# Block attention and a feed-forward layer on one core: score and product tiles of one PSUM bank each, and four smaller edits of the plan

## The chip, the cores and the metric

The kernel runs on 1 core of one Trainium2 chip. The metric is device time in microseconds. The time before is 644.97 us, the median of 3 runs (643.79 to 647.47).

## The reference

Two stages follow each other. The first is attention with a local window and block summaries, over 4 batches, 8 heads, 768 positions and 64 features; the second is a feed-forward layer on the 3072 tokens that come out.

```python
block, window = (32, 16)
k_sum = k.reshape(B, H, nb, block, D).max(axis=3)
v_sum = v.reshape(B, H, nb, block, D).mean(axis=3)
scores_l = where(|i - j| < window, scale * q @ k.T, -1e9)
scores_s = scale * q @ k_sum.T + log(block)
a = softmax(concat([scores_l, scores_s]))          # 1e-9 is added to the sum
x = a @ concat([v, v_sum])                         # then (tokens, 512)
h = x @ w_in                                       # 512 -> 2048
g = h * erf(softplus(h))
out = g @ w_out                                    # 2048 -> 512
```

Everything is float32.

## The kernel before, in words

**Tiling.** The 3072 tokens go in 6 chunks of 512. A chunk needs 4 quads of attention (a quad is one pair of heads over 512 tokens, 24 quads in all, numbered `qd`) and 4 periods of the feed-forward layer (a period is 512 of the 2048 inner features, 24 periods in all, numbered `k`; `g = k % 4` is the group of inner features). Attention for quad `k + 4` or so runs inside period `k`, so that TensorE always has feed-forward work beside it. Multiplications of the feed-forward layer are made in three passes: both operands are split into a high and a low part of type fp32r, and high x high, high x low and low x high are added in PSUM.

**Attention of one quad.** `scores` (line 543) fills two PSUM banks, one for each head of the pair; `softmax` (line 581) has VectorE add the mask (line 589, both banks in one instruction) and take the maximum, ScalarE the exponentials with their sums (line 605), and VectorE normalise (line 621); `transp` (line 627) transposes eight 128 x 120 pieces on TensorE into the same two banks, and ScalarE copies both to SBUF in one instruction (line 639); `av` (line 650) multiplies by the values; `xsplit` or `xsplit_fast` splits the result into high and low parts.

**The feed-forward layer in periods 0 to 7.** `mm1` makes `h`, `hout` copies it, then come the activation (softplus; in the first four periods tanh and a logarithm), `erfs` (line 883, the erf, two instructions of 128 x 1024), `gsplit` (line 888: the product at 898, the high part, the low part at 905) and `mm2` (line 910), which multiplies period `k - 1`'s `g` by `w_out` while period `k` is being made. In periods 4 to 7 the erfs are told to come after that period's exponentials (line 1145).

**From period 8 on.** `products` (line 792) makes `h` with fewer multiplications, after Strassen: seven block products, P1 to P7, for each of two halves `n`, from weights, sums of weight blocks (`add_up`) and sums of token blocks (`tsplit`). A job of `products` is six matmuls of 256 columns. The jobs go out in the order P1a P1b P2a P2b P6a P5a P6b P5b P7a P3a P7b P3b P4a P4b, where the last letter is the half: a for the first, b for the second. The first half's results stand in two PSUM tiles of one bank, `h0` and `h1`; the second half's in one PSUM tile of two banks, `pa` (its banks are called pA and pB in the plan). In a pair the first bank takes P2, P5 and P3, the second P1, P6, P7 and P4. Results are copied or added to `hc` as they come: out1, out6, out5, out7 (line 858), out3 (line 861) and out4. In the profile a job of the first half appears as `ha` or `hb`, one of the second half as `pa`.

**Weights.** Sums of weight blocks are made once in periods 5 to 7, in the order of groups 1, 2, 3, 0 (`add_up`, line 387): eight instructions of 128 x 512 for a group (lines 394 and 397), each on VectorE or GpSimd as the plan finds it free; ScalarE and VectorE then split them (403 and 406), and they are stored to device memory. From period 7 on they come back by `get_sums` (line 428, 1 MB each), and the split `w_out` by `get` (line 369, 1 MB each): four such transfers in a period, through a ring of five SBUF slots.

**What sets the order.** Each step is put down as an operation with a cost for each engine that can do it and with names that it reads and writes (`Plan.add`, line 62). `Plan.order` (line 103) is a list scheduler: it takes the engine that can start first and, of the operations that are ready there, the one with the smallest key. The key is a due time, to which a table (`TUNE`, line 46) adds a number for operations 0 to 463; for some operations the table also names the engine. TensorE may take an operation out of turn up to 60 places ahead, as long as its place is below 330, and after that follows the program. `hold` puts off the moment at which a transfer counts as ready in the plan. The instructions of each engine, and of SyncE, which issues almost all transfers, are written out in the planned order, and each engine runs its own list in that order. The semaphores between engines are added afterwards by the tile framework, from the tiles that instructions read and write.

**Draining.** Every fourth period `evac` (line 932) copies a finished chunk from the four output banks to SBUF, on ScalarE alone, and SyncE stores it. Three of the four homes of these copies are the SBUF rows into which `load_nat` loads keys and values for the block summaries.

## Time and profile before

| | |
|---|---|
| runs | 643.79, 644.97, 647.47 us |
| profiled execution, its own time | 646.77 us |
| its span, first to last instruction | 645.0 us |
| mean granted TensorE clock | 0.995 |
| VectorE busy | 432.1 us (67%) |
| ScalarE busy | 406.7 us (63%) |
| GpSimd busy | 39.7 us (6%) |
| moved by DMA | 150.23 MB, 233 GB/s on average |

Everything below the second row is from the profiled execution. A page of the profile has the busy time of each engine, and for each group of instructions their count, mean duration and the idle time of the engine before them, with what ended it. In the profile PE is TensorE's matmuls, PEld its weight loads (which overlap the matmuls), DVE is VectorE, ACT ScalarE, POOL GpSimd and SPq the queue of SyncE. A line such as `PE pa L808 <- DVE hc L861` says that a matmul of line 808 that writes `pa` waited for an instruction of VectorE at line 861 that writes `hc`; a number in brackets at the end of a timeline row is the engine's idle time before it. Line 278 is the helper that copies, so it appears for many tiles. The recorded duration of a matmul includes its way through the array; how often matmuls start is what counts for time, and for those of 256 columns that is every 0.12 us where nothing waits.

### The profile page before, as it was taken

The numbers are of one execution on the slowest core, as the hardware profiler recorded it, in microseconds if no ns is written. First come the engines' busy times: TensorE is split into PE (matmuls) and PEld (weight loads), VectorE is DVE, ScalarE is ACT, GpSimd is POOL, SyncE is SP. The second block draws the span as 40 slices with busy tenths as digits, with TensorE's granted clock in tenths as the row PEclk, the third lists the DMA queues.
The fourth block names the chain that finished last, engine by engine and source line by source line (L and its number), as shares of the span: only waits on it lengthen the run. The fifth ranks groups of instructions, "written<-read, shape, count | busy, mean of one in ns | idle before, by whom it ended". The sixth has DMA issues, their size and how long they took to land.

```text
span 645.0 us, 12021 instructions
## 1 busy us (share of the span) xinstructions
PE 622.7 (97%) x4840; PEld 522.6 (81%) x4840; DVE 432.1 (67%) x607; ACT 406.7 (63%) x804; POOL 39.7 (6%) x68
## 2 busy tenths in 40 slices
PE   7999999999899998999989999999999999999997
PEld 5776558888688787888879889898888898889886
DVE  4999999745898984865658656557646475424442
ACT  5679977887968684664564674574675555552450
POOL 2011010100132310000000000000000000000000
PEclk9999999999899998999999999999999999999999
DMA  9998948734675978788756776666587555574611
GB/s 318 257 381 289 347 163 268 249 109 143 228 275 171 351 246 323 251 296 277 272 171 225 273 259 217 244 218 216 216 271 256 190 181 184 196 258 147 240 74 65
DMA packets 36843, 150.23 MB, mean 233 GB/s; under 512 B 3956, under 2 KB 9396, under 8 KB 24244
## 3 DMA queue, kind: packets, MB, share of 16 engines
q1 hardware_dynamic: 36212, 148.95, 67.4%
q8 instruction: 38, 0.62, 0.4%
q10 hardware_dynamic: 576, 0.52, 0.2%
q14 instruction: 17, 0.14, 0.1%
HBM read 124.13 MB, written 23.07 MB: 228 GB/s over the span
## 4 chain that ended last, share of the span: by engine, by line
PE 78%; DVE 11%; DMA 5%; ACT 3%; issue 1%; SPq 0%; DVEq 0%; ACTq 0%
PE ops L922 31%; PE pa L808 12%; PE h L763 11%; PE hb L808 5%; PE ha L808 5%; PE ops L918 4%; PE px L660 3%; PE pa L635 3%; PE pa L564 2%; DMA out<-rows 2%; DVE hc L861 1%; DVE hc L898 1%; DMA rows<-k_nat 1%; DMA rows<-v_nat 1%; DVE hc L858 1%
## 5 line engine op out<-in xcount | busy, mean ns | idle before, releaser
L922 PE MATMUL ops<-w,gh 128*128 128x512 f32 x704 | 229.7, 395 | 0.0
L922 PEld LDWEIGHTS ops<-w,gh 128*128 128x128 f32 x704 | 132.8, 189 | 27.2 <-ACT gh L278 0.2
L922 PE MATMUL ops<-w,gl 128*128 128x512 f32 x352 | 137.6, 391 | 1.0 <-DVE gl L905 1.0
L898 DVE TENSOR_TENSOR hc<-wt,hc 128x1024 f32<-128x1024 f32 x44 | 55.3, 1273 | 69.6 <-ACT wt L886 69.6
L1169 ACT ACT_TABLE_LOAD x76 | 97.5, 1283 | 1.4
L763 PE MATMUL h<-xh,w 128*128 128x512 f32 x256 | 86.9, 405 | 0.3 <-ACT hc L278 0.3
L922 PEld LDWEIGHTS ops<-w,gl 128*128 128x128 f32 x352 | 66.3, 188 | 13.6 <-DVE gl L905 1.3
L278 ACT COPY hc<-hb 128x256 f32<-128x256 f32 x35 | 13.1, 373 | 85.9 <-PE hb L808 50.1
L763 PEld LDWEIGHTS h<-xh,w 128*128 128x128 f32 x256 | 48.6, 190 | 12.7 <-ACT hc L278 1.5
L605 ACT ACTIVATE pr<-pr,stats 128x120 f32<-128x120 f32 x128 | 48.8, 382 | 8.6 <-DVE stats L614 8.4
L905 DVE TENSOR_TENSOR gl<-hc,gh 128x1024 fp32r<-128x1024 f32 x44 | 53.5, 1222 | 0.3
L763 PE MATMUL h<-xl,w 128*128 128x512 f32 x128 | 50.2, 393 | 0.0
L886 ACT ACTIVATE wt<-wt 128x1024 f32<-128x1024 f32 x48 | 50.0, 1058 | 0.3
L278 DVE CAST gh<-hc 128x1024 fp32r<-128x1024 f32 x40 | 27.8, 697 | 23.5 <-PE ops L922 23.2
L808 PE MATMUL pa<-w,ws 128*128 128x256 f32 x288 | 41.0, 287 | 0.8 <-DVE hc L278 0.8
L527 POOL COPY kw<-ksum 128x96 f32<-128x96 f32 (+1 forms) x28 | 16.1, 590 | 397.9 <-DMA kw<-k_win 270.6
L808 PEld LDWEIGHTS pa<-w,ws 128*128 128x128 f32 x288 | 37.4, 194 | 1.3 <-DVE hc L278 1.2
L808 PE MATMUL hb<-w,ws 128*128 128x256 f32 x192 | 29.1, 288 | 4.3 <-ACT hc L278 2.7
L278 ACT CAST xh<-px 128x512 fp32r<-128x512 f32 (+1 forms) x20 | 10.2, 512 | 36.0 <-PE px L660 36.0
L874 ACT ACTIVATE wt<-hc 128x1024 f32<-128x1024 f32 x32 | 32.1, 1052 | 0.2
L808 PEld LDWEIGHTS hb<-w,ws 128*128 128x128 f32 x192 | 25.9, 196 | 4.7 <-ACT hc L278 2.9
L918 PE MATMUL ops<-a32s,gw 128*128 128x512 f32 x64 | 29.2, 595 | 0.0
(168 smaller groups left out, 1099.0 us busy)
## 6 DMA issues: line engine op xcount, KB each, us to landing
w<-dr SPq DMA_DIRECT2D x36, 1024.0 KB
ws<-ds SPq DMA_DIRECT2D x30, 1024.0 KB
kw<-k_win SPq DMA_DIRECT2D x20, 480.0 KB
rw<-w_in SPq DMA_DIRECT2D x8, 1024.0 KB
rw<-w_out SPq DMA_DIRECT2D x8, 1024.0 KB
dr<-w SPq DMA_DIRECT2D x8, 1024.0 KB
ds<-ws SPq DMA_DIRECT2D x8, 1024.0 KB
vw<-v_win SPq DMA_DIRECT2D x20, 384.0 KB
```

The source lines that it names most:

```text
L278: e.copy(o, i) if e is nc.scalar else e.tensor_copy(o, i)
L605: nc.scalar.activation(s["pr"][:, j], s["pr"][:, j] if qd >= MQ else s["sc"][j // NI][:, i * NK:(i + 1) * NK], AF.Exp, scale=0.125, bias=s ...
L635: nc.tensor.transpose(tp[0:NK, a, i * 128:(i + 1) * 128], s["pr"][:, NI * a + i], ident)
L763: nc.tensor.matmul(hs[k, f][:, 0:T], lhsT=w[m], rhs=xt[ch, cc][x], start=(cc == 0 and n == 0), stop=(cc == 3 and n == 2))
L808: nc.tensor.matmul(shape, lhsT=w[m], rhs=y[l], start=first and c == 0 and i == 0, stop=c == 1 and i == 2, skip_group_check=True)
L874: nc.scalar.activation(wt[k, n], hc[k, n], AF.Softplus)
L886: act(0.96, lambda n=n: nc.scalar.activation(wt[k, n], wt[k, n], AF.Erf, scale=-1.0 if k < SOFT else 1.0), [s], [s], table=("sig",), after ...
L898: e.tensor_tensor(hc[k, n], wt.pop((k, n)), hc[k, n], op=ALU.mult)
L905: e.tensor_tensor(gs[k, n][1], hc.pop((k, n)), f32(gs[k, n][0]), op=ALU.subtract)
L918: nc.tensor.matmul(os_[ch, t], lhsT=x[0][:, i % 2, t * 128:(t + 1) * 128], rhs=w32["o", g, i // 2][:, i % 2], start=first, stop=last)
L922: nc.tensor.matmul(os_[ch, t], lhsT=x[y][:, i % 2, t * 128:(t + 1) * 128], rhs=w[m], start=first and n == 0, stop=last and n == 2)
L1169: nc.scalar.preload_act_table_set(sets[o["load"]])
```

## The change

Five edits are made together. (1) `pa` becomes two PSUM tiles of one bank each, pA and pB, for scores, transposes and the second half's products. The mask is then added in two instructions and the transposed pieces are copied in two; the plan's costs for these steps go from 1.07 to 1.2 and from 0.9 to 1.1. The first job in the second half's second bank claims that bank alone in the plan, not both. (2) The sums of weight blocks are made by VectorE alone for groups 0 and 2 and by GpSimd alone for groups 1 and 3, with a planned cost of 1.5 on GpSimd in place of 1.3. (3) The two kinds of streamed weights, `get` and `get_sums`, have a hold of 2.0 in place of 0. (4) `evac` may run on ScalarE or VectorE, with costs of 0.59 and 0.69 in place of 0.45. (5) The erfs of periods 4 to 7 are no longer told to wait for the exponentials. The table of keys stays as it is.

```diff
@@ -63,7 +63,6 @@
 
 
         n, deps = len(self.ops), set(after)
-        r, w = ([y for x in z for y in (("pA", "pB") if x == "pa" else (x,))] for z in (r, w))
         for x in r:
             deps.update(self.last.get(x, ()))
         for x in w:
@@ -203,7 +202,7 @@
         return t if len(shape) == 2 else t.rearrange("p (a b) -> p a b", a=shape[1]) if len(shape) == 3 else t.rearrange("p (a b c) -> p a b c", a=shape[1], b=shape[2])
 
     def ps(name, tag):
-        return psum.tile([128, 2, 512] if tag == "pa" else [128, 512], F32, name=name, tag=tag)
+        return psum.tile([128, 512], F32, name=name, tag=tag)
 
     ident = sb([128, 128], F32, "ident")
     make_identity(nc, ident)
@@ -287,6 +286,7 @@
     FIRST = {4: 9, 5: 8, 6: 12, 7: 13}
     LATER = {0: 12, 1: 13, 2: 9, 3: 8, 4: 9, 5: 8}
     ROUND = (12, 13, 11, 9, 8)
+    ON_DVE = (0, 2)
     SUMS, TURN, RAW_X = 11, (12, 13), 10
     kept = {}
 
@@ -374,7 +374,7 @@
             t = slot(n, [128, 2, 2, 512], F32R, "w")
             whl[u] = t[:, 0], t[:, 1]
             nc.sync.dma_start(out=f32(t), in_=dr[m])
-        dma(1049, go, [f"d{m}"], frees(n), hold=0.0)
+        dma(1049, go, [f"d{m}"], frees(n), hold=2.0)
 
 
     w_at = {("o", m // 2, m % 2): n for m, n in FIRST.items()}
@@ -408,7 +408,7 @@
         def out_(n):
             dr["s", g, n] = dram.tile([128, 2, 4, 2, 128], F32, name=f"ds{g}{n}", tag=f"ds{g}{n}")
             nc.sync.dma_start(out=dr["s", g, n], in_=f32(s["hl", n]))
-        sum_eng = {"DVE": 0.66, "POOL": 1.3}
+        sum_eng = {"DVE": 0.66} if g in ON_DVE else {"POOL": 1.5}
         for i, (r, j) in ((0, (0, 0)), (3, (1, 1)), (2, (0, 1)), (1, (1, 0))):
             on(sum_eng, lambda e, i=i, r=r, j=j: whole(e, i, r, j), w[r:r + 1] + ([] if i == 0 else [f"w{SUMS}"]), (frees(SUMS) if i == 0 else []) + [f"s{i}"])
         for o, x, y, op in ((3, 2, 3, ALU.add), (2, 0, 2, ALU.subtract), (0, 3, 0, ALU.subtract), (1, 1, 0, ALU.subtract)):
@@ -431,7 +431,7 @@
         def go():
             t = w_sum[g, n] = slot(m, [128, 2, 4, 2, 128], F32R, "ws")
             nc.sync.dma_start(out=f32(t), in_=dr["s", g, n])
-        dma(1049, go, [f"ds{g}{n}"], frees(m), hold=0.0)
+        dma(1049, go, [f"ds{g}{n}"], frees(m), hold=2.0)
 
 
     rows = sb([128, 2 * S], F32, "rows")
@@ -540,15 +540,16 @@
             dma(100 if n == NB else 50, lambda b=b, js=js, n=n: nc.sync.dma_start(out=s["vw"][LW:NK, js], in_=vsum[vrows[b % 2], p:p + 1, :].to_broadcast([NS, n, 128])),
                 [f"vsum{b % 2}{p}"], ["vw"])
 
-    def scores(qd, banks=("pa",)):
+    PA = ("pA", "pB")
+
+    def scores(qd, banks=PA):
 
         s = st[qd]
 
         def mask():
             for n in banks:
                 tiles[n] = ps(n, n)
-            s["sc"] = [tiles["pa"][:, 0], tiles["pa"][:, 1]] if banks == ("pa",) else [tiles[n] for n in banks]
-            s["both"] = tiles["pa"] if banks == ("pa",) else None
+            s["sc"] = [tiles[n] for n in banks]
             m0 = mask_at[qd // NP % 3]
             for sc in s["sc"] if qd < MQ else []:
 
@@ -578,7 +579,7 @@
             pe(0.96, lambda: keys(near), [f"qf{qd}", f"kf{qd}"], banks)
             pe(0.5, lambda: keys(lambda r, j: [(LW, ksum[r, 0, qd])]), [f"qf{qd}", f"ksum0{qd}"], banks)
 
-    def softmax(qd, banks=("pa",)):
+    def softmax(qd, banks=PA):
         s = st[qd]
         m0 = mask_at[qd // NP % 3]
         mk = mask_sb[:, m0:m0 + NI]
@@ -586,8 +587,8 @@
 
         def add(e):
             t = s["pr"] = sb([128, 2 * NI, NK], F32, "pr")
-            e.tensor_tensor(t.rearrange("q (a i) c -> q a i c", a=2), s["both"][:, :, 0:NI * NK].rearrange("q a (i c) -> q a i c", i=NI),
-                            mk.unsqueeze(1).to_broadcast([128, 2, NI, NK]), op=ALU.add)
+            for a in range(2):
+                e.tensor_tensor(t[:, NI * a:NI * a + NI], s["sc"][a][:, 0:NI * NK].rearrange("q (i c) -> q i c", i=NI), mk, op=ALU.add)
 
         def red(e):
             s["mx"] = stat(0, par)
@@ -609,7 +610,7 @@
             e.tensor_scalar(s["rs"], s["sm"], 1e-9, None, op0=ALU.add)
 
         if qd >= MQ:
-            on({"DVE": 1.07}, add, banks, [pr])
+            on({"DVE": 1.2}, add, banks, [pr])
         on({"DVE": 1.06 if qd >= MQ else 1.14}, red, [pr] if qd >= MQ else banks, [f"mx{par}"])
         on({"DVE": 0.07}, lambda e: e.tensor_scalar(s["mx"], s["mx"], -0.125, None, op0=ALU.mult), [f"mx{par}"], [f"mx{par}"])
         s["exps"] = act(3.02 if qd >= MQ else 2.7, exps, [f"mx{par}"] + ([] if qd >= MQ else list(banks)), [pr, f"sm{par}"], table=("log", "exp"))
@@ -629,16 +630,17 @@
         pr = "pr" if qd >= NP else f"pr{qd}"
 
         def go():
-            tp = tiles["pa"] = s["tp"] = ps("pa", "pa")
+            s["tp"] = [ps(n, n) for n in PA]
             for a in range(2):
                 for i in range(NI):
-                    nc.tensor.transpose(tp[0:NK, a, i * 128:(i + 1) * 128], s["pr"][:, NI * a + i], ident)
+                    nc.tensor.transpose(s["tp"][a][0:NK, i * 128:(i + 1) * 128], s["pr"][:, NI * a + i], ident)
 
         def cp():
             s["pt"] = sb([NK, 2, T], F32, "ptr", "pt")
-            nc.scalar.copy(s["pt"], s["tp"][0:NK, :, 0:T])
-        pe(0.95, go, [pr], ["pa"])
-        act(0.9, cp, ["pa"], ["pt"])
+            for a in range(2):
+                nc.scalar.copy(s["pt"][:, a], s["tp"][a][0:NK, 0:T])
+        pe(0.95, go, [pr], PA)
+        act(1.1, cp, PA, ["pt"])
 
     turned = [0]
 
@@ -787,7 +789,7 @@
         act(0.96 if k < SOFT else 1.06, fn, [f"hc{s}"], [f"wt{s}"], table=("sig", "exp") if k < SOFT else ("soft",))
 
     def pair_banks(n):
-        return ("h0", "h1") if n == 0 else ("pA", "pB")
+        return ("h0", "h1") if n == 0 else PA
 
     def products(k):
         ch, g = divmod(k, NG)
@@ -795,11 +797,7 @@
 
         def go(n, x, what, z, first):
             if (n, x) not in where_:
-                if n == 0:
-                    where_[0, x] = ps("h" + x, pair_banks(0)["ab".index(x)])
-                else:
-                    t = tiles["pa"] = ps("pa", "pa")
-                    where_[1, "a"], where_[1, "b"] = t[:, 0], t[:, 1]
+                where_[n, x] = ps("h" + x, pair_banks(n)["ab".index(x)])
             o = where_[n, x][:, z]
             for c in range(2):
                 w, y = what(n, c)
@@ -837,7 +835,7 @@
 
         def job(name, n):
             x, what, z, first, r = jobs[name]
-            pe(0.72, lambda: go(n, x, what, z, first), r(n), pair_banks(n) if (name, n) == ("P1", 1) else [pair_banks(n)["ab".index(x)]])
+            pe(0.72, lambda: go(n, x, what, z, first), r(n), [pair_banks(n)["ab".index(x)]])
 
         def bank(n, x):
             return where_[n, x]
@@ -932,10 +930,10 @@
     def evac(ch, t):
         home = HOMES[t]
 
-        def cp():
+        def cp(e):
             tiles["ob", t] = rows[:, t * C:t * C + C] if t < 3 else sb([128, C], F32, "ob", "mask_h")
-            nc.scalar.copy(tiles["ob", t], os_.pop((ch, t)))
-        act(0.45, cp, [f"o{t}"], home)
+            copy(e, tiles["ob", t], os_.pop((ch, t)))
+        on({"ACT": 0.59, "DVE": 0.69}, cp, [f"o{t}"], home)
         dma(262, lambda: nc.sync.dma_start(out=out[ch * T + t * 128:ch * T + (t + 1) * 128], in_=tiles["ob", t]), home)
 
     def evac_last(t):
@@ -952,7 +950,7 @@
         on({"DVE": 0.4}, lambda e: go(e, 1), [f"o{t}"], after=[len(P.ops) - 1])
 
 
-    banks = [("pa",), ("h0", "h1"), ("o0", "o1"), ("h0", "h1")]
+    banks = [PA, ("h0", "h1"), ("o0", "o1"), ("h0", "h1")]
     idle = ps("idle", "o3")
 
     def busy(n):
@@ -1142,7 +1140,7 @@
             for r in range(2):
                 get(2 * (k % NG) + r, turn())
         logs(k)
-        erfs(k, [st[qs]["exps"]] if NG <= k < FAST and qs < NQ else [])
+        erfs(k, [])
         if k and g == 0:
             for t in range(NT):
                 evac(ch - 1, t)
```

## The prediction

> **What bounds the kernel now.** I read the page's busy times first.
>
> ```profile
> PE 622.7 (97%) x4840; PEld 522.6 (81%) x4840; DVE 432.1 (67%) x607; ACT 406.7 (63%) x804; POOL 39.7 (6%) x68
> ```
>
> TensorE bounds it: 645.0 us of span hold 22.3 us in which no matmul is recorded. None of the edits takes matmuls away, so only such gaps, and stretches at a lower clock, can be won. Next the waits of TensorE's weight loads, which show a gap sooner than the matmuls (columns: total us, times, longest).
>
> ```profile
> PEld pa L808 <- DVE hc L861: 10.1, 14, 1.2
> PEld hb L808 <- ACT hc L278: 2.9, 1, 2.9
> PEld hb L808 <- DVE hc L278: 1.7, 1, 1.7
> ```
>
> The first is nearly half of it all and comes back 14 times: a product of the second half waits for out3. The others come once each, and the table by stretch (us, PE busy, PEld, DVE, ACT, POOL, clock, DMA share, GB/s) shows where.
>
> ```profile
> 30.00:60.00 30.00, 30.00 (x213) 21.36 (x209) 29.48 (x37) 25.10 (x54) 4.07 (x4) 1.00 0.94 339
> 160.00:185.00 25.00, 22.54 (x150) 17.94 (x149) 20.67 (x28) 23.62 (x45) 5.42 (x5) 0.93 0.73 258
> 215.00:245.00 30.00, 27.30 (x195) 22.88 (x193) 28.25 (x36) 21.84 (x39) 3.83 (x4) 1.00 0.85 313
> 245.00:271.40 26.40, 26.08 (x207) 23.32 (x208) 15.72 (x23) 16.06 (x35) 0.35 (x1) 0.94 0.82 277
> 474.40:499.30 24.90, 24.43 (x206) 21.70 (x206) 14.33 (x22) 14.88 (x33) 1.25 (x1) 1.00 0.78 266
> ```
>
> An early stretch (30 to 60) has no gap. Around 160 to 185 TensorE stands for 2.46 us and runs the rest at a mean clock of 0.93 over the stretch; at 215 to 271.4 it is 2.70 + 0.32 us and 0.94. A late period loses about half a microsecond and nothing else. So there are two places to win: the wait in every late period, and two stalls in periods 4 to 8.
>
> **Part 1: the split tile.** One late period in order of time:
>
> ```profile
> 478.53 0.88 PE L808 MATMUL hb<-w 128*128 128x256 f32 x6
> 478.80 0.42 DVE L858 TENSOR_TENSOR hc<-pa,hc 128x256 f32<-128x256 f32 x1 [0.82 <-PE pa L808]
> 479.14 0.68 DVE L861 TENSOR_TENSOR hc<-pa,hc 128x512 f32<-128x512 f32 x1
> 479.87 0.98 PE L808 MATMUL pa<-w 128*128 128x256 f32 x6 [0.47 <-DVE hc L861]
> ```
>
> P4a (`hb<-w`) starts at 478.53, and its six matmuls at 0.12 us leave TensorE free at 479.25. P4b writes bank pB. The last reader of pB is out7 (line 858), which ends at 479.22. Yet P4b starts at 479.87, 0.05 us after out3 (line 861) ended at 479.82, and out3 reads pA. That is a wait for a reader of the other bank, and it costs 0.62 us. Whether two tiles of one bank have it can be read off the first half, which has such tiles already:
>
> ```profile
> 328.07 0.88 PE L808 MATMUL hb<-w 128*128 128x256 f32 x6
> 328.62 0.68 DVE L861 TENSOR_TENSOR hc<-ha,hc 128x512 f32<-128x512 f32 x1
> ```
>
> There P4a starts 0.55 us before the out3 of its own half, so nothing holds it. After the change P4b then waits for out7 alone. In the late period out7 ends 0.03 us before TensorE is free, and it can only come sooner: it now starts after P3b, the last writer of the old tile, and will need P7b alone. I leave no rest of this wait. Its price is 10.1 us less the 0.05 us by which the weight load's gap exceeds the true loss (0.67 in this row's period against 0.62), 14 times: 10.1 - 0.7 = **9.4 us**, with 8.7 (14 x 0.62) and 10.1 as bounds.
>
> What the split adds are second instructions:
>
> ```profile
> L639 ACT COPY ptr<-pa 120x1024 f32<-120x1024 f32 x24 | 24.1, 1006 | 5.0 <-PE pa L635 3.6 <-PE px L660 1.4
> L278 ACT COPY hc<-h 128x512 f32<-128x512 f32 x22 | 12.6, 594 | 13.3 <-PE h L763 13.2
> L589 DVE TENSOR_TENSOR pr<-pa,mask_sb 128x960 f32<-128x960 f32 x16 | 18.4, 1151 | 6.8 <-PE pa L564 6.8
> L660 PEld LDWEIGHTS px<-ptr,vw 120*64 120x64 f32 x640 | 20.3, 138 | 4.4 <-issue 2.9 <-ACT w L278 0.8 <-ACT pr L605 0.4
> ```
>
> The copy becomes two of some 0.59 us: 1.19 - 1.01 = 0.18 us, 24 times, 4.3 us of ScalarE. The mask becomes two of about 0.65 us (out3's 0.68 us is for 512 columns, these are 480): 0.15 us, 16 times, 2.4 us of VectorE. The last row shows that the product after the copy never waits for line 639, so the matmuls put between them cover it; uncovered it would be 4.3 us. Queued behind the longer mask on VectorE are the maximum and the next results' copies, in late periods with VectorE busy 14 of 25 us. I charge 0.4 us, for the first quads, where little lies between; bounds 0 and 4.3.
>
> **Part 2: the erfs of periods 4 to 7.** ScalarE, and what TensorE made of it, in period 4:
>
> ```profile
> 149.11 1.06 ACT L781 ACTIVATE wt<-hc 128x1024 f32<-128x1024 f32 x1 [0.64 <-DVE hc L278]
> 156.30 0.59 ACT L937 COPY rows<-ops 128x512 f32<-128x512 f32 x1 [1.89 <-PE ops L922]
> 163.12 2.00 ACT L886 ACTIVATE wt<-wt 128x1024 f32<-128x1024 f32 x2
> 168.56 0.79 PE L922 MATMUL ops<-w,gl 128*128 128x512 f32 x1 [0.95 <-DVE gl L905]
> ```
>
> The softplus is done at 150.2, the erf starts at 163.1, after the exponentials, and five microseconds later TensorE gets the low part of `g` that it stands for. In between ScalarE idled (1.89 us in the second row alone). Without the order the planner finds the erfs ready some 10 us sooner, and a list scheduler takes what is ready. The stall is worth 2.46 us and, by the clock, up to 0.07 x 25.0 = 1.75 us: 4.2 us at most, nothing at least. I take **3.0**, since the two readings of one slow stretch overlap. A greedy order may run the first erf between the two softplus and pay two more table loads in a period; in period 4 the idle time of ScalarE covers them. Period 7 is the second stall:
>
> ```profile
> 225.70 1.06 ACT L781 ACTIVATE wt<-hc 128x1024 f32<-128x1024 f32 x1
> 230.29 1.05 ACT L403 CAST ws<-sums 128x1024 fp32r<-128x1024 f32 x1 [2.24 <-DVE sums L397]
> 239.01 2.01 ACT L886 ACTIVATE wt<-wt 128x1024 f32<-128x1024 f32 x2
> 245.32 0.98 PE L808 MATMUL hb<-w,ws 128*128 128x256 f32 x6 [2.73 <-ACT hc L278]
> ```
>
> It is the same pattern, 12 us from softplus to erf, but here VectorE is busy 28.25 of 30 us, so an earlier erf meets a full queue. The stall is worth 2.70 + 0.32 + 0.06 x 26.4 = 4.6 us. I take **1.5**: a third, because VectorE has to work off the same list by the same time.
>
> **Part 3: sums by one engine.** Of 32 instructions GpSimd has 12 now, and gets 16:
>
> ```profile
> L394 POOL TENSOR_TENSOR sums<-w 128x512 f32<-128x512 f32 x7 | 10.7, 1539 | 31.8 <-DVE ws L406 18.1 <-DVE w L352 13.7
> L397 POOL TENSOR_TENSOR sums<-sums 128x512 f32<-128x512 f32 x5 | 8.2, 1634 | 9.8 <-DVE sums L397 9.6
> 211.09 4.37 POOL L397 TENSOR_TENSOR sums<-sums 128x512 f32<-128x512 f32 x2 [2.11 <-DVE sums L397]
> 211.99 4.55 DVE L898 TENSOR_TENSOR hc<-wt,hc 128x1024 f32<-128x1024 f32 x2
> L898 DVE TENSOR_TENSOR hc<-wt,hc 128x1024 f32<-128x1024 f32 x44 | 55.3, 1273 | 69.6 <-ACT wt L886 69.6
> ```
>
> VectorE loses four of about 0.68 us (out3's duration for as many columns), 2.7 us less. But the rows at 211 and 212 show both engines slow beside each other: two of line 898 take 4.55 us, against 2 x 1.27 by their mean. So a GpSimd instruction beside VectorE costs it about 1.0 us, and four more cost 4.0. Net it is -2.7 to +1.3 us of VectorE; I set it at nothing and carry 4.0 as a bound on what reaches TensorE.
>
> **Part 4: streamed weights later, and the drain.** SyncE and the first use of what it fetched, and one transfer of 256 KB from the chain of waits:
>
> ```profile
> 427.44 0.34 SPq L433 DMA_DIRECT2D ws<-ds  x1
> 428.88 8.87 SPq L376 DMA_DIRECT2D w<-dr  x2
> 447.85 0.88 PE L808 MATMUL hb<-w,ws 128*128 128x256 f32 x6
> 277.01 8.71 DMA out<-rows
> ```
>
> The sums asked for at 427.44 are used after 447.85. A megabyte takes about 3.9 us at the 266 GB/s of the late stretch, and even a small transfer in a crowd took 8.71, so more than 10 us stay. A hold moves these issues behind other transfers in SyncE's queue, not behind anything that TensorE stands for: **0**, bounds -1 and +1. The drain, free to take VectorE, releases the rows sooner, and late rows made this:
>
> ```profile
> 293.67 0.95 DVE L452 TENSOR_REDUCE vs_sum<-rows 128x24 f32<-128x768 f32 x1 [3.54 <-DMA rows<-v_nat]
> 296.55 0.98 PE L808 MATMUL hb<-w,ws 128*128 128x256 f32 x6 [1.54 <-DVE hc L278]
> ```
>
> The reduction held VectorE's queue for 3.54 us, and TensorE lost 1.54. I take 0.5 of it; bounds 1.7 and nothing.
>
> **The sum.** 9.4 + 3.0 + 1.5 + 0.5 - 0.4 = 14.0 us. The profiled execution took 646.77 us, 1.77 more than its span, and becomes 632.8. It lies 1.80 above the median of the runs, so the median becomes 644.97 - 14.0 = **631.0 us**.
>
> **The rivals.** *The wait goes, the stalls only move.* A planner that is given other costs writes another order for periods 4 to 11, and DVE's 28.25 of 30 us speak for a stall of the same size elsewhere. Then only 9.4 less 0.4, 9.0, is left: 644.97 - 9.0 = 636.0 us. Chance 0.24.
>
> *VectorE and GpSimd in each other's way.* Group 3 on GpSimd alone is eight instructions in a chain, 12.6 us at the mean of the twelve (18.9 / 12 = 1.58) and 17.5 at the 2.19 of the row at 211.09, and group 0 queues behind it, where VectorE is full. If all of the 4.0 us lands on TensorE and nothing is won in the middle, it is 644.97 - 9.0 + 4.0, that is 640.0 us. Chance 0.06. The Trainium skill, in SBUF — State Buffer, under "Who interferes with whom", states that a VectorE instruction with two SBUF inputs and a GpSimd instruction that reads SBUF shut each other out for a whole instruction. By that rule, the two rows at 211 and 212 agree: both sides were stretched.
>
> *The split changes no wait.* If the semaphores were still set by the pair, all that part 1 wins is lost, and 3.0 + 1.5 + 0.5 - 0.4 = 4.6 is won: 640.4 us. The row at 328.07 speaks against it. Chance 0.03.
>
> *Slower: the new order opens gaps in the stretch that has none.* Copies and masks cost more in the plan from the first quad on, and an early stretch now has 30.00 of 30.00 us. A stall of the kind at 160 to 185 costs 4.2 us with its clock. The 9.0 us of part 1 pay for two; three make 12.6 - 9.0 = 3.6 us more than now, and from there on the kernel is slower: 648.6 us. Against it: the table of keys and the steps themselves stay. Chance 0.05.
>
> **How the numbers follow.** The forecast has the remaining 0.62. The range starts at 644.97 - 10.1 - 4.2 - 4.6 - 1.7 + 0.4, about 625 us, with every bound on the good side, and ends at 640, which takes in the first rival and reaches the second; beyond lie the slow rival and the third. A measurement of this kernel can tell about 0.5%, 3.2 us, from no change. Faster by more than that (below 641.7) are the forecast, the first rival and most of the next two: 0.91; within it 0.04; slower 0.05.
>
> **What would show it.** The row PEld pa <- DVE hc L861 is gone or below 1 us in total, P4b follows P4a by 0.72 us, and late periods last 24.3 in place of 24.9. The erf of period 4 starts before the exponentials, and stretch 160 to 185 has a clock above 0.97. Line 639 has 48 copies of about 0.59 us with no TensorE wait on them. The prediction is wrong if P4b waits for another reader, or if periods 4 to 8 hold more than 5.5 us of gaps (now 2.46 + 2.70 + 0.32).

## The result and the profile after

The changed kernel takes 628.73 us, the median of 4 runs (626.72 to 631.60). The kernel before, on the same chip, takes 645.04 us (643.79 to 647.47). The ratio is 0.9746, with a 95% interval from 0.9698 to 0.9794: 16.3 us faster. The profiled execution took 629.01 us, with a span of 627.2 us and a clock of 0.997; the four runs differ by the clock that they were granted, 1.000 for 626.72 us, 0.997 for 628.44 and 629.01, 0.995 for 631.60. Lines have moved by one to three: the products are now line 806 (808 before), out3 is 859 (861), out7 856 (858), the erf 884 (886), the copy helper 277 (278), the output products 920 (922).

The busy times of the changed kernel, from its page:

```profile
PE 618.2 (99%) x4840; PEld 520.9 (83%) x4840; DVE 440.3 (70%) x634; ACT 409.6 (65%) x820; POOL 46.4 (7%) x72
```

TensorE now lacks 9.0 us of its span (627.2 - 618.2); before it lacked 22.3. The waits of its weight loads in the changed kernel (total us, times, longest), the largest that has a releaser and the only one of a product that is over 0.2 us:

```profile
PEld ops L920 <- DMA w<-dr: 2.9, 1, 2.9
PEld ha L806 <- DVE w L743: 1.0, 1, 1.0
```

The row with 14 waits and 10.1 us is gone, and so are both waits of `hb` for copies of `hc`. The first row is new: an output product that waited 2.9 us for a weight transfer. In place of `pa`, the products now write `ha` and `hb` in both halves. The two product jobs that the prediction followed, in a late period of the changed kernel's timeline:

```profile
465.35 0.42 DVE L856 TENSOR_TENSOR hc<-hb,hc 128x256 f32<-128x256 f32 x1
465.80 1.60 PE L806 MATMUL hb<-w 128*128 128x256 f32 x12
466.00 0.69 DVE L859 TENSOR_TENSOR hc<-ha,hc 128x512 f32<-128x512 f32 x1 [0.23 <-PE ha L806]
```

P4a and P4b are one row of twelve matmuls without a break, 1.60 us long, and out3 runs beside them from 466.00 to 466.69. The seventh of them, the first of P4b, starts at 466.52, before out3 has ended. In the row that the prediction shows of before, P4a started at 478.53 and P4b ended at 480.85: 2.32 us for the same work. That is 0.72 us a period. The table by stretch of the changed kernel (us, PE busy, PEld, DVE, ACT, POOL, clock, DMA share, GB/s):

```profile
30.00:60.00 30.00, 29.86 (x206) 21.06 (x206) 29.57 (x37) 24.19 (x50) 2.74 (x4) 1.00 0.92 338
160.00:185.00 25.00, 25.00 (x170) 20.62 (x169) 21.54 (x29) 21.81 (x41) 10.40 (x9) 1.00 0.67 232
215.00:245.00 30.00, 28.98 (x221) 25.10 (x219) 26.80 (x39) 22.56 (x42) 2.95 (x3) 1.00 0.85 289
245.00:271.40 26.40, 23.90 (x188) 20.95 (x189) 16.86 (x29) 15.21 (x34) 0.84 (x1) 0.94 0.84 296
461.00:485.20 24.20, 24.20 (x207) 21.67 (x206) 14.70 (x24) 14.79 (x35) 0.63 (x1) 1.00 0.78 268
```

The early stretch stayed full but for 0.14 us. The stall of period 4 is gone, with its clock. The stall between 215 and 271 is not: it is 1.02 + 2.50 us of gap there, 3.02 before, and the clock of the stretch from 245 on is 0.94 again. A late period is 24.20 us and full. In period 4 the first erf now stands between the two softplus and both stand ahead of the exponentials (the last row is the first exponential's sum):

```profile
150.26 1.06 ACT L884 ACTIVATE wt<-wt 128x1024 f32<-128x1024 f32 x1
155.26 1.06 ACT L884 ACTIVATE wt<-wt 128x1024 f32<-128x1024 f32 x1
157.93 0.19 ACT L606 ACTIVATION_READ_ACCUMULATOR pr<-pr,stats 128x1 f32 x1
```

The new stall, first on TensorE, then in the chain of waits of the changed kernel:

```profile
247.50 0.50 PE L920 MATMUL ops<-w,gh 128*128 128x512 f32 x1 [2.73 <-DMA w<-dr]
```

```profile
237.67 1.15 DVE ws L406
238.87 8.58 DMA w<-dr
```

A part of `w_out` is fetched into the ring's slot 11. That slot holds the weight sums of group 0 until their second low part is split off (line 406), which ends at 238.82. SyncE issues the transfer at 238.87, and it lands 8.58 us later, while TensorE stands. In the kernel before the same transfer was issued at much the same time, 239.59, but TensorE stood for the erf then, and needed the weights only later.

### The profile page after: what moved, and what is told of

Its sections match the earlier page's. It is cut to its first block, busy times and chain, and to the rows that moved or that the text cites. A ratio compares the mean times of both kernels' runs of the same rounds, so it can differ in the third digit from the quotient of the medians.

```text
span 627.2 us, 12062 instructions
## 1 busy us (share of the span) xinstructions
PE 618.2 (99%) x4840; PEld 520.9 (83%) x4840; DVE 440.3 (70%) x634; ACT 409.6 (65%) x820; POOL 46.4 (7%) x72
## 4 chain that ended last, share of the span: by engine, by line
PE 91%; DVE 5%; DMA 1%; ACT 1%; issue 1%; SPq 0%; DVEq 0%
PE ops L920 37%; PE hb L806 14%; PE h L765 13%; PE ha L806 10%; PE ops L916 4%; PE px L662 4%; PE pA L565 3%; PE pA L636 2%; PE pB L636 1%; DMA w<-dr 1%; PE idle L959 1%; ACT prf L606 1%; DVE ws L406 1%; DVE gl L903 1%; DVE sums L397 0%
## 5 line engine op out<-in xcount | busy, mean ns | idle before, releaser
L277 ACT COPY hc<-hb 128x256 f32<-128x256 f32 x49 | 18.1, 373 | 95.4 <-DVE hc L859 40.4
L806 PE MATMUL hb<-w,ws 128*128 128x256 f32 x384 | 56.8, 283 | 0.0
L903 DVE TENSOR_TENSOR gl<-hc,gh 128x1024 fp32r<-128x1024 f32 x44 | 54.8, 1246 | 0.8
L806 PEld LDWEIGHTS hb<-w,ws 128*128 128x128 f32 x384 | 50.7, 192 | 0.2 <-DVE ws L406 0.2
L765 PE MATMUL h<-xl,w 128*128 128x512 f32 x128 | 49.9, 390 | 0.0
L277 DVE CAST gh<-hc 128x1024 fp32r<-128x1024 f32 x43 | 30.0, 698 | 18.1 <-PE ops L920 16.9
L277 DVE COPY hc<-hb 128x256 f32<-128x256 f32 x47 | 19.8, 422 | 15.2 <-PE hb L806 13.9
L806 PE MATMUL ha<-w,ws 128*128 128x256 f32 x192 | 28.5, 283 | 0.8 <-DVE w L743 0.8
L856 DVE TENSOR_TENSOR hc<-hb,hc 128x256 f32<-128x256 f32 x32 | 13.5, 422 | 22.3 <-PE hb L806 20.7
```

What stands on the lines that cost most here:

```text
L277: e.copy(o, i) if e is nc.scalar else e.tensor_copy(o, i)
L765: nc.tensor.matmul(hs[k, f][:, 0:T], lhsT=w[m], rhs=xt[ch, cc][x], start=(cc == 0 and n == 0), stop=(cc == 3 and n == 2))
L806: nc.tensor.matmul(shape, lhsT=w[m], rhs=y[l], start=first and c == 0 and i == 0, stop=c == 1 and i == 2, skip_group_check=True)
L903: e.tensor_tensor(gs[k, n][1], hc.pop((k, n)), f32(gs[k, n][0]), op=ALU.subtract)
```

## The experiments

Twelve kernels, four at a time, each beside the kernel before on the same chip (its medians there: 644.74, 644.14 and 644.97 us). So a difference of less than about 1 us between kernels of different groups says nothing. Four columns of the table come from the profiled runs: the time between the starts of two of TensorE's 1120 matmuls that write the output tiles, counted from the first; every trace has all 1120. The 97th to the 193rd take in the stall of period 4, the 241st to the 385th that of periods 7 and 8, the 385th to the 481st the one at 296 us that the prediction puts down to late rows, and the 481st to the 1057th are twelve late periods. (The expectations write the fourth, seventh and eighth period for periods 4, 7 and 8.) What is left out is the same everywhere (25.0 us from the 193rd to the 241st, 18.2 after the 1057th), but for the start: the 97th comes at 124.6 to 127.3 us.

| kernel | median us | ratio, 95% interval | 97th-193rd | 241st-385th | 385th-481st | 481st-1057th |
|---|---|---|---|---|---|---|
| before | 645.04 |   | 58.2 | 79.4 | 53.0 | 285.5 |
| changed | 628.73 | 0.9746 (0.9698-0.9794) | 53.9 | 79.9 | 48.5 | 276.6 |
| tile divided alone | 629.44 | 0.9766 (0.9735-0.9797) | 54.9 | 75.3 | 49.8 | 276.6 |
| tile divided, old order | 632.35 | 0.9816 (0.9778-0.9854) | 58.4 | 78.6 | 48.5 | 276.6 |
| undivided, P4b later | 633.55 | 0.9831 (0.9808-0.9854) | 57.2 | 78.7 | 50.5 | 276.9 |
| all but the tile | 637.92 | 0.9913 (0.9882-0.9944) | 53.8 | 80.3 | 50.5 | 285.5 |
| erfs free alone | 636.59 | 0.9869 (0.9845-0.9893) | 53.8 | 76.8 | 49.9 | 285.5 |
| tile divided, erfs free | 629.92 | 0.9776 (0.9730-0.9822) | 53.9 | 76.1 | 53.9 | 276.6 |
| changed, erfs held | 634.83 | 0.9850 (0.9826-0.9875) | 61.5 | 77.7 | 48.5 | 276.6 |
| changed, slots 11 and 9 swapped | 624.33 | 0.9690 (0.9652-0.9729) | 53.9 | 75.1 | 48.5 | 276.6 |
| changed, no later fetches | 625.88 | 0.9716 (0.9672-0.9761) | 53.9 | 75.7 | 48.5 | 276.6 |
| changed, sums on any engine | 625.26 | 0.9699 (0.9675-0.9723) | 53.9 | 75.2 | 48.5 | 276.6 |
| changed, output copies on ScalarE | 627.30 | 0.9734 (0.9710-0.9759) | 53.9 | 76.5 | 48.5 | 276.6 |
| changed, swapped and no later fetches | 626.02 | 0.9705 (0.9681-0.9729) | 53.9 | 75.1 | 49.6 | 276.6 |

The last column falls into two groups with nothing between them: 285.5 us where P4b waits, 276.6 to 276.9 where it doesn't. The profile of "all but the tile" is of an execution 4.4 us longer than its median, and its 80.3 holds a slow stretch of the clock after a gap of 2.03 us, so that figure is not typical of the kernel.

### What the divided tile does

**The tile divided alone.** The first edit of the change, nothing else:

```diff
-        return psum.tile([128, 2, 512] if tag == "pa" else [128, 512], F32, name=name, tag=tag)
+        return psum.tile([128, 512], F32, name=name, tag=tag)
```

> The kernel before with the first edit alone: scores and the second pair's products in two tiles of one bank, everything else as it was. Theory (the output products waited for a tile that is read twice, and all of that wait is exposed): the wait of P4b goes in all 14 periods that show it, 0.72 us each by the lengths of the late periods of the two profiles (24.9 to 24.2), so about 635 us (645.0 less 10.1), the row of weight loads of P4b waiting for the output's second block product is gone, and the rest of the gain, some 6 us, is missing. Rival (the tile only allowed another order, and the gain comes from the exponentials and erfs that follow each other without being held): most of the 16 us is missing, 641 us or more, and the late periods stay at 24.9.

Measured: 629.44 us, 15.3 us less than the kernel before on that chip, where the whole change has 16.3. The theory was right on the late periods (8.9 us less between the 481st and the 1057th) and wrong in holding that nothing else would come: the early periods gained as well, 10.7 us in the other three columns. (Its profile and that of the kernel before are further apart than the medians.) The stretch of period 4 and, from the timeline, its erfs in this kernel:

```profile
160.00:185.00 25.00, 24.66 (x165) 20.05 (x164) 21.76 (x29) 22.89 (x39) 4.59 (x4) 1.00 0.69 243
```

```profile
159.95 2.01 ACT L884 ACTIVATE wt<-wt 128x1024 f32<-128x1024 f32 x2
```

The erfs are still held behind the exponentials, but everything came 3.2 us sooner (159.95 against 163.12), and TensorE lost 0.34 us there, not 2.46. Two causes were mixed in this kernel: another order, because the planner's costs and claims changed with the tile, and tiles that are handed over bank by bank.

**The tile divided, in the old order.** The planner's numbers were put back, so that every operation keeps its engine and its place. In the traces the instructions of TensorE, VectorE, ScalarE and GpSimd follow in the order of the kernel before, with one more behind each mask and each copy of transposed pieces:

```diff
-            on({"DVE": 1.2}, add, banks, [pr])
+            on({"DVE": 1.07}, add, banks, [pr])
...
-        act(1.1, cp, PA, ["pt"])
+        act(0.9, cp, PA, ["pt"])
...
-            pe(0.72, lambda: go(n, x, what, z, first), r(n), [pair_banks(n)["ab".index(x)]])
+            pe(0.72, lambda: go(n, x, what, z, first), r(n), pair_banks(n) if (name, n) == ("P1", 1) else [pair_banks(n)["ab".index(x)]])
```

> The kernel before with the tile divided, but with the planner's costs and claims as they were, so that every engine gets its work in the order of the kernel before (each mask add and each transposed copy is now two instructions in a row). This sets apart the two things that the split alone did in 629.4 us: the false wait, and another order. Theory: the wait of P4b goes, 14 times 0.72 us, and nothing else: about 635 us, with the stalls of the fourth period (some 5 us by the windows) and of the second block products behind ScalarE (4.4 us) still there. Rival (the order has no part in it, bank-wise handing over frees the early stalls too): 629 to 631 us.

Measured: 632.35 us. The stretch of period 4 and TensorE's largest wait in this kernel:

```profile
160.00:185.00 25.00, 22.92 (x150) 17.98 (x149) 20.73 (x29) 23.47 (x45) 5.43 (x5) 0.93 0.74 267
```

```profile
PE hb L806 <- ACT hc L277: 2.8, 1, 2.8
```

Both early stalls are where they were in the kernel before. So the tile by itself is worth 11.8 us (ratio 0.9816), more than the 10.1 of the theory but well short of the whole, and the stalls went in the kernel above because the order was another one. What the theory left out is the stall of 296.55, which is gone too: 4.5 us between the 385th and the 481st, of which two periods' waits of P4b are 1.4. The same stretch before and in this kernel:

```profile
295.00:300.00 5.00, 3.46 (x28) 3.29 (x28) 4.82 (x9) 3.30 (x18) 0.35 (x1) 1.00 0.97 312
295.00:300.00 5.00, 5.00 (x44) 5.00 (x44) 3.34 (x8) 1.12 (x3) 0.00 (x0) 1.00 0.90 272
```

VectorE waits 0.9 us for the rows there, not 3.54, though no step has another place. Why they come in time is not shown. That the order is worth the remaining 2.9 us of the medians is less sure than the place, since the two intervals overlap and the two kernels ran on different chips.

**The wait covered, not removed.** The two-bank tile stays. Half of the output products that came after P4b are put ahead of it:

```diff
+            if name == "P4b":
+                mm2(k - 1, (0,), (0, 1))
...
-            mm2(k - 1, (0,))
+            mm2(k - 1, (0,), (2, 3))
```

> The kernel before, two-bank tile kept, with half of the output's matmuls for the first weight block (the first two of four row tiles) put ahead of P4b instead of behind it. The computation is whole. Theory (P4b waits only because the other half of its tile is still being read, for well under 2 us): the products put ahead cover the wait, the row of P4b's wait goes though the tile is undivided, and the time is near that of the split, 635 us, or a little above it for what the later P4b makes late (637). Rival (P4b's wait is only the place where TensorE stands, and VectorE is late for everything behind it): the wait turns up at the next reader and the time stays at 643 us or more.

Measured: 633.55 us. A late period in this kernel:

```profile
470.07 0.88 PE L808 MATMUL hb<-w 128*128 128x256 f32 x6
470.34 0.42 DVE L858 TENSOR_TENSOR hc<-pa,hc 128x256 f32<-128x256 f32 x1 [0.82 <-PE pa L808]
470.68 0.68 DVE L861 TENSOR_TENSOR hc<-pa,hc 128x512 f32<-128x512 f32 x1
472.17 0.88 PE L808 MATMUL pa<-w 128*128 128x256 f32 x6
```

Between P4a and P4b TensorE does output products; out3 ends at 471.36, and P4b starts at 472.17 without a wait. Of the row of P4b's waits one is left, of 0.4 us. The late periods are as short as with the divided tile, to 0.3 us (276.9 against 276.6). So VectorE was late for nothing that comes behind P4b, and with the old order above, the wait was for the other bank's reader: it can be taken away by dividing the tile, or filled with other work, and the late periods gain the same.

### What the erfs do

**Erfs free alone,** on the kernel before:

```diff
-        erfs(k, [st[qs]["exps"]] if NG <= k < FAST and qs < NQ else [])
+        erfs(k, [])
```

> The kernel before with the last edit alone: the erfs of the early periods are no longer put behind the exponentials. Theory (the erfs held TensorE up in the fourth period for 4.9 us, and in the seventh for less): 640 us, with the erfs of the fourth period starting near 150 and 155 us instead of 163. Rival (the planner had put them late for want of ScalarE's time, not for the rule): 645 us and the erfs where they were.

Measured: 636.59 us, 3.4 better than the theory. Of this kernel, the first erf of period 4, the stretch, and the weight loads that still wait at P4b:

```profile
150.49 1.06 ACT L886 ACTIVATE wt<-wt 128x1024 f32<-128x1024 f32 x1
```

```profile
160.00:185.00 25.00, 25.00 (x170) 20.63 (x169) 23.25 (x33) 23.09 (x51) 4.74 (x4) 1.00 0.83 282
```

```profile
PEld pa L808 <- DVE hc L861: 10.8, 15, 1.3
```

Period 4 gains 4.4 us (58.2 to 53.8), periods 7 and 8 gain 2.6 (79.4 to 76.8), and 3.0 came between the 385th and the 481st, where nothing was expected: no wait for rows is left there. The late periods keep their wait.

**All but the tile:** the kernel before with the change's other four edits.

```diff
-        sum_eng = {"DVE": 0.66, "POOL": 1.3}
+        sum_eng = {"DVE": 0.66} if g in ON_DVE else {"POOL": 1.5}
...
-        erfs(k, [st[qs]["exps"]] if NG <= k < FAST and qs < NQ else [])
+        erfs(k, [])
```

> The kernel before with all edits but the first: the two-bank tile is kept, sums by one engine per group, weights and sums asked for 2 us later, the output's copies on either engine, erfs of the early periods not held behind the exponentials. Theory: the late periods keep their 24.9 us and the wait of P4b its row of about 10 us; the stall of 4.9 us in the fourth period goes, so about 639 us. Rival (the rest carries the gain): 634 us or less.

Measured: 637.92 us, as the theory had it, with P4b's row still there:

```profile
PEld pa L809 <- DVE hc L862: 11.4, 16, 1.2
```

The other three edits add nothing to the erfs' (637.92 against 636.59 us, with intervals that overlap).

**The tile divided and erfs free,** both edits on the kernel before:

```diff
+    PA = ("pA", "pB")
...
-        erfs(k, [st[qs]["exps"]] if NG <= k < FAST and qs < NQ else [])
+        erfs(k, [])
```

> The divided tile and the erfs not held, nothing else of the change. By adding the two single gains (15.3 and 8.2 us) it would be 621 us. Theory (both take away the same stalls of the early periods, by different orders; only P4b's wait is the split's own): no better than the split alone, 627 to 631 us. Rival (the gains add): 624 us or less.

Measured: 629.92 us. The gains don't add: 15.3 and 8.2 alone, 14.2 together. The table shows why: but for the wait of P4b, both take the same stalls away, wholly or in part. Together, one stall came back, first on VectorE and then on TensorE:

```profile
290.10 0.95 DVE L452 TENSOR_REDUCE vs_sum<-rows 128x24 f32<-128x768 f32 x1 [5.18 <-DMA rows<-v_nat]
292.04 0.98 PE L806 MATMUL hb<-w,ws 128*128 128x256 f32 x6 [3.69 <-DVE hc L277]
```

VectorE stood 5.18 us for rows from memory with a copy queued behind, the same pattern that cost the kernel before 1.54 us. TensorE lost 3.69 us here, and the clock was then 0.50 from 293.1 to 296.5, another 1.7.

**The changed kernel with the erfs held again:**

```diff
-        erfs(k, [])
+        erfs(k, [st[qs]["exps"]] if NG <= k < FAST and qs < NQ else [])
```

> The changed kernel without its fifth edit: the erfs of the early periods held behind the exponentials again. My sum in the prediction gave the edit 4.5 us, so 633 us. Theory after the first seven runs (the divided tile lets the order hide those erfs anyway): no worse than the changed kernel, 626 to 630 us, or faster if the late weight block of the eighth period is gone with the other order.

Measured: 634.83 us, 6.1 slower than the changed kernel. The theory of that expectation fell; the prediction's sum came near the number, 633, but not for its reason. Period 4 is the worst of all kernels (61.5). In this kernel, GpSimd, VectorE and TensorE there:

```profile
161.70 7.40 POOL L394 TENSOR_TENSOR sums<-w 128x512 f32<-128x512 f32 x4 [5.16 <-DVE w L352]
161.74 4.56 DVE L896 TENSOR_TENSOR hc<-wt,hc 128x1024 f32<-128x1024 f32 x2
166.34 1.65 DVE L277 CAST gh<-hc 128x1024 fp32r<-128x1024 f32 x1
170.24 0.80 PE L920 MATMUL ops<-w,gl 128*128 128x512 f32 x1 [2.57 <-DVE gl L903]
```

And the kernel with the tile divided alone, where the first sums go to GpSimd after these steps of VectorE:

```profile
161.04 2.36 DVE L896 TENSOR_TENSOR hc<-wt,hc 128x1024 f32<-128x1024 f32 x2 [1.24 <-ACT wt L884]
163.51 0.69 DVE L277 CAST gh<-hc 128x1024 fp32r<-128x1024 f32 x1
168.11 2.56 POOL L394 TENSOR_TENSOR sums<-w 128x512 f32<-128x512 f32 x2 [11.46 <-DVE w L352]
```

The chain from the erf to the low part of `g` is what TensorE waits for. Its two gaps there are 1.19 and 2.57 us, and the clock is 0.50 from 169.6 to 176.5, which costs another 3.4: 7.2 of the 7.6 us by which this stretch is longer than in the changed kernel. Beside GpSimd its product takes 2.28 us and not 1.18, and the cast 1.65 and not 0.69; GpSimd's own instruction takes 1.85 us and not 1.28. With the erfs late, the whole group of sums on GpSimd falls beside this chain. That is the second rival of the prediction, seen at work, though not in the changed kernel: there the erfs are early and the same sums run from 166.20 at 1.26 us each, when nobody waits. That GpSimd is the cause is read from these durations; with the erfs held, no run moved the sums alone. For the product it agrees with the Trainium skill, SBUF — State Buffer, under "Who interferes with whom": a VectorE instruction with two SBUF inputs and a GpSimd one that reads SBUF exclude each other. The cast has one input, and that sentence says nothing of it.

### What the changed kernel still loses

**Slots 11 and 9 swapped** in the order in which the ring's slots are taken:

```diff
-    ROUND = (12, 13, 11, 9, 8)
+    ROUND = (12, 13, 9, 11, 8)
```

> The changed kernel with the weight block that TensorE needs first in the eighth period put into the ring's slot 9, which comes free earlier, instead of slot 11, which waits for the second low split of a group of sums. Theory (the late transfer costs 2.7 us of wait and some 1.3 us of slower matmuls behind it): the row of output products waiting for a weight transfer goes, about 625 us. Rival (the block that takes slot 11 is then late in its turn, or the order finds another stall): 628 to 630 us.

Measured: 624.33 us (623.65 to 625.46), the fastest kernel here; its slowest run is faster than the fastest of the changed kernel, though the intervals of the two ratios overlap. No wait for a weight transfer is left, and the largest wait of a product is this one:

```profile
PE hb L806 <- ACT hc L277: 0.9, 1, 0.9
```

Periods 7 and 8 take 75.1 us in place of 79.9. So the late block cost more than its 2.73 us of standing; most of the rest is the clock, below.

**No later fetches:** streamed weights and sums asked for as early as before.

```diff
-        dma(1049, go, [f"d{m}"], frees(n), hold=2.0)
+        dma(1049, go, [f"d{m}"], frees(n), hold=0.0)
...
-        dma(1049, go, [f"ds{g}{n}"], frees(m), hold=2.0)
+        dma(1049, go, [f"ds{g}{n}"], frees(m), hold=0.0)
```

> The changed kernel with streamed weights and sums asked for as early as before (no 2 us later). Theory (the 2 us only leave time that the transfers don't need, or cost a little where a ring slot comes free late): the same within 1 us, 628 to 629.5 us, perhaps 2 us faster if the late weight block of the eighth period comes earlier for it. Rival (asking later keeps transfers out of each other's way): 631 us or more.

Measured: 625.88 us (625.66 to 626.58), 2.8 below the changed kernel's median. The intervals of the two ratios overlap; in the profiles periods 7 and 8 take 75.7 us in place of 79.9. In this kernel TensorE's wait at the same place, and that transfer in the chain of waits:

```profile
245.72 0.50 PE L920 MATMUL ops<-w,gh 128*128 128x512 f32 x1 [0.18 <-DMA w<-dr]
```

```profile
239.65 6.04 DMA w<-dr
```

The transfer is issued 0.8 us later than in the changed kernel and lands 1.8 us sooner: 6.04 us on the way, not 8.58.

**Sums on any engine,** the second edit undone:

```diff
-        sum_eng = {"DVE": 0.66} if g in ON_DVE else {"POOL": 1.5}
+        sum_eng = {"DVE": 0.66, "POOL": 1.3}
```

> The changed kernel without its second edit: each weight sum goes to whichever of VectorE and GpSimd the order finds free, as in the kernel before. Theory (my estimate: the sums' engine is worth nothing, within 4 us): 627 to 630 us if the late weight block of the eighth period stays late, 624 to 626 us if the ring's slot of the sums comes free earlier for it. Rival (sums spread over both engines hold VectorE up, and one engine per group is where part of the gain lies): 631 us or more.

Measured: 625.26 us, on the good side of the theory. The wait for the late block is gone, and GpSimd has ten of the sums. Slot 11 came free only 0.75 us sooner than in the changed kernel (238.07 against 238.82), and the transfer landed before the products needed it at 244.02:

```profile
L394 POOL TENSOR_TENSOR sums<-w 128x512 f32<-128x512 f32 x7 | 10.8, 1567 | 38.8 <-DVE ws L406 28.8 <-DVE w L352 10.1
L397 POOL TENSOR_TENSOR sums<-sums 128x512 f32<-128x512 f32 x3 | 4.7, 1555 | 3.8 <-DVE sums L397 3.1 <-DVE sums L394 0.7
```

**Output copies on ScalarE alone,** the fourth edit undone:

```diff
-            copy(e, tiles["ob", t], os_.pop((ch, t)))
-        on({"ACT": 0.59, "DVE": 0.69}, cp, [f"o{t}"], home)
+            nc.scalar.copy(tiles["ob", t], os_.pop((ch, t)))
+        act(0.45, cp, [f"o{t}"], home)
```

> The changed kernel without its fourth edit: the output's copies on ScalarE alone. Theory (0.5 us at the drain by my sum): 628 to 630 us. Rival (ScalarE is full around the periods in which outputs are copied, and the erfs are late behind the copies): 631 us or more.

Measured: 627.30 us (626.16 to 629.38), not to be told from the changed kernel. Here too the late block came nearly in time, by the timeline and the chain of waits:

```profile
247.30 0.50 PE L920 MATMUL ops<-w,gh 128*128 128x512 f32 x1 [0.47 <-DMA w<-dr]
```

```profile
240.93 6.32 DMA w<-dr
```

**Swapped, and no later fetches:** the two diffs above together.

```diff
+    ROUND = (12, 13, 9, 11, 8)
...
+        dma(1049, go, [f"d{m}"], frees(n), hold=0.0)
```

> The two variants that were faster than the changed kernel put together: the first-needed weight block in slot 9, and weights and sums asked for as early as before. Theory (both take away the same wait for one late weight block): no gain over the better of the two, 623 to 626 us. Rival (two different losses): 621.5 us or less.

Measured: 626.02 us, no better than either: both take away one and the same wait. What follows from these five: no price of its own can be given for the second, third or fourth edit. Undoing any one gave a lower median, and in each the block that slot 11 keeps waiting does less harm, because its transfer is quicker. Why it took 8.58 us in one kernel and 6.0 to 6.3 in others stays open. With early fetches the four engines' instructions have the changed kernel's order up to 257 us; what differs before that is the order of SyncE. In the changed kernel a store of 1 MB was issued 0.4 us behind the transfer, with early fetches 3.9 us behind, with sums on any engine 3.8; but with the copies on ScalarE it was 0.4 us behind as well, and the transfer took 6.32.

## Why the prediction was right

The forecast was 631.0 us and the time is 628.73, inside the range, with the largest term the one that the prediction had. Its steps:

**The wait of P4b** (9.4 us, bounds 8.7 to 10.1). Right in mechanism, shown by two kernels, the divided tile in the old order and the undivided one with P4b later, that have no more in common than that P4b does not stand. The size was too small. In the changed kernel P4b always starts 0.72 us after P4a, in the kernel before 0.75 to 1.87 us after. The fifteen excesses of its trace come to 9.5 us, and with 0.10 us for each restart to 11.0; the last twelve are the 8.9 us of the table. The step that failed is "less the 0.05 us by which the weight load's gap exceeds the true loss". I measured the loss to the start of P4b's matmuls. But its row of before says that these six took 0.98 us, where six without a wait take 0.88 (the first row of the same fence): the loss is 0.62 + 0.10, and the weight load's gap was the better number. Taking this one period for all left out two earlier ones, in which out3 was later and P4b stood 1.15 and 0.83 us.

**The erfs of period 4** (3.0 of at most 4.2). The full bound came: 4.4 us between the 97th and the 193rd matmul in the kernel with that edit alone and in the changed kernel. It is not the edit's alone, for the other order that came with the tile took 3.4 of it with the erfs still held. The step that failed is "the two readings of one slow stretch overlap": the gaps, 1.51 us up to 166.13 and 0.95 up to 168.56, and the clock of 0.50 from 168.4 to 171.8 are two losses, one after the other.

**The erfs of period 7** (1.5 of at most 4.6). The term's own reading was that VectorE has to work off the same list by the same time. It didn't hold: 2.6 us came alone, and 4.3 (79.4 to 75.1) with the slots swapped, 0.7 of that from a P4b. But the divided tile without the edit has as much (75.3). In the changed kernel nothing was won there (79.9), for the stall only moved, to a weight transfer. That is the first rival, true for one of the two stalls.

**The second instructions** (0.4). The rows of the changed kernel:

```profile
L641 ACT COPY ptr<-pA 120x512 f32<-120x512 f32 x24 | 13.8, 576 | 5.4 <-PE pA L636 4.2 <-PE px L662 1.1
L641 ACT COPY ptr<-pB 120x512 f32<-120x512 f32 x24 | 14.3, 594 | 0.0
L591 DVE TENSOR_TENSOR pr<-pA,mask_sb 128x480 f32<-128x480 f32 x16 | 10.4, 652 | 7.4 <-PE pB L565 7.4
```

The durations are those of the sum, 1.17 us for a copy and 1.30 for a mask, and no row of TensorE's waits names them. So no run shows the 0.4 us.

**Sums by one engine** (0, bound 4.0) and **fetches later** (0, bounds -1 and +1). The medians with one of them undone are lower, by 3.5 and 2.8 us, with intervals that overlap. In the second's profile the gain is 4.2 us in periods 7 and 8, past the bound; the step that failed is "not behind anything that TensorE stands for". The transfer that TensorE stood for was issued 0.05 us after its slot came free, so the hold did not put it off; it let a store go out close behind, and whether that slowed the transfer stays open. For the sums the bound held, but what came was not what had been priced, GpSimd and VectorE beside each other: it was that late transfer. The rows of GpSimd in the changed kernel:

```profile
202.71 7.33 POOL L394 TENSOR_TENSOR sums<-w 128x512 f32<-128x512 f32 x4 [2.97 <-DVE ws L406]
210.01 7.24 POOL L397 TENSOR_TENSOR sums<-sums 128x512 f32<-128x512 f32 x4
```

That is the chain of 14.6 us that the second rival had between 12.6 and 17.5. What the rival made of it, 640.0 us, needed VectorE's chain beside it.

**The drain** (0.5). Not shown to be worth anything: undone, it made no difference that these runs can tell. The stall that the term was part of, TensorE's wait behind late rows, is gone in the changed kernel (48.5 us between the 385th and the 481st), but just so with this edit undone and with the tile alone in the old order.

**The sum.** Terms taken from one profile were added as if each edit kept the rest of the order as it was. They don't add: 15.3 and 8.2 us alone, 14.2 together. Between the two profiles the spans differ by 17.8 us: 11.0 from P4b, 4.4 in period 4, 3.1 from the stalls at 296 and just behind, 0.5 before the 97th matmul, and 1.2 lost in periods 7 and 8 apart from P4b. The forecast had 9.4, 3.0, 0.5, -0.4 and +1.5 for these. So four terms were too small, by 6.5 us in all, and one too large by 2.7. That the total came within 2.3 us of the median is in part luck. The start of the table's kernels differs by as much as 2.7 us, so the 0.5 says little. The range's low end also left out two bounds on the good side, 1 us for the fetches and nothing for the second instructions; with them it would be about 623 us. *The split changes no wait* is refuted by the missing row, *slower* by the time and by the early stretch, in which TensorE is busy 29.86 of 30 us.

## What to carry to other kernels

Under this tile framework the PSUM tile of two banks, read bank by bank, made its writers wait for readers of the other bank: look for a wait whose releaser reads an address that the waiting instruction does not write, and divide the tile or fill the wait with work that is there anyway. Price a wait of TensorE from the end of the instruction before to the end of the one that waited, less what the same work takes without a wait. Where a list scheduler writes the order, an edit's worth is known only together with that order: run it alone and undone before saying what it is worth, and look at which buffer comes free last once the old stalls are gone.

## What the runs showed of the hardware

**The clock after a short gap.** In the changed kernel TensorE stood 2.73 us up to 247.50. Four rows by microsecond after it (250 to 251 has 0.50 as well):

```profile
248.00:249.00 1.00, 1.00 (x6) 0.79 (x5) 0.00 (x0) 0.98 (x2) 0.00 (x0) 0.99 0.89 377
249.00:250.00 1.00, 1.00 (x4) 0.78 (x3) 0.00 (x0) 0.99 (x2) 0.00 (x0) 0.50 0.41 172
251.00:252.00 1.00, 1.00 (x4) 0.70 (x4) 1.00 (x1) 0.00 (x0) 0.00 (x0) 0.50 0.69 205
252.00:253.00 1.00, 1.00 (x9) 1.00 (x8) 0.13 (x1) 0.38 (x1) 0.00 (x0) 0.81 0.91 385
```

The clock is halved from about 249.0 to 252.4, well after the gap was over. Some 3.4 us at half speed cost 1.7 us, so the stall cost 4.4 in all; the swap of the slots gained 4.4 us of the median. Between 160 and 300 us, the traces of all kernels have eight such stretches of 3.4 us and one of twice that, all at 0.50. The shortest single gap with one behind it is 2.03 us, in the kernel with all but the tile; behind the 1.54 us at 296.55 in the kernel before there is none. One stretch lowers the mean clock of the whole execution by 0.003 (1.7 of 627 us), so the run of the changed kernel with a mean clock of 1.000 had none: an estimate, since only one run of each kernel was profiled. The Trainium skill, TensorE: Matmul & The Clock Gate, under "What's actually happening", has the clock halved after an idle window of about 3.4 us. The length of the slow stretch agrees with that window; that a gap of 2.73 us was enough does not.

**A restart.** The first six matmuls after a wait took 0.98 us, and 0.88 without one. The 0.10 us lie between the first and the second, 0.22 us apart in place of 0.12, in all fifteen P4b of the kernel before. At 479.87 the first weight load and the first matmul start together; for P4a, which did not wait, the load starts 0.12 us ahead (478.41 and 478.53).
